# Eight zero fills that leave out one transfer engine in place of six, and four fills moved

## The chip, the cores and the metric

The kernel runs on one core of a Trainium2 chip. The metric is the device time of one launch in microseconds (us), here the median of several runs. The profiles show instructions of five engines (PE, here for matrix products, DVE, ACT, POOL and SP) and count transfers as a share of 16 transfer engines; in the kernel before these moved 248.19 MB, with 61.87 MB read from HBM and 185.60 MB written to it. All comparisons are between runs in the fast state, and the mean clock that the profiled runs were granted differs little (0.733 to 0.747 of full speed).

## The reference, cut to what matters

The program computes a decoder block with a modulated layer norm, attention over the last 4096 positions of a 65,536-long key and value cache, and a gated feed-forward part (FFN), and then all its gradients. The gradients of the two caches are nearly all zeros:

```python
k = jnp.repeat(k_cache[:, :, Sk - W:, :], rep, axis=1)   # W = 4096 of Sk = 65536
v = jnp.repeat(v_cache[:, :, Sk - W:, :], rep, axis=1)
# ... attention, FFN ...
_out, _vjp = jax.vjp(_f, A_x, A_k_cache, A_v_cache, A_wq, ...)
_grads = _vjp(grad_out)     # dK and dV have the caches' full size; rows before Sk - W are zero
```

So the kernel must write 2 x 4 x 61,440 x 128 zeros in bf16. That is 120 pieces of 1 MB (128 rows of 8 KB each), about half of all that it moves. Nothing waits for these zeros, so they can be written at any time.

## The kernel before

Python lists say how many zero fills are issued at which place. `NARROW` says which fills, by their index in the order of issue, are narrow.

```python
SKIP = 4
NARROW = (8, 20, 40, 65, 90, 104)
Z_Q = [0] * 7 + [3]                    # after the products of q, tile j
Z_N = spread(29, 128)                  # N stage, paced by PE and DVE
Z_B = spread(29, 43) + [1, 1, 1, 1, 0] # B stage, paced by PE
Z_FOLD = (3, 4)
Z_FFN = [(1, 1, 1, 1)] * 6 + [(1, 2, 1, 1)]   # seven FFN blocks, four places each
Z_END = (3, 1, 1, 1, 1)                # gradient stage at the end; what is left comes last
...
def zero(n, after=None):
    for _ in range(n):
        ...
        region, narrow_ = zleft.pop(0)
        if narrow_:
            nc.gpsimd.inc_swdge_sem([], [], mode="reset_dge_cursor")
            ...
            first = nc.gpsimd.dma_start(      # NS = SKIP + 1 = 5 rows: ten packets of 256 bytes
                out=rest[0:NS, ...], in_=zeros[0:NS, 0:64]...)
            ins = nc.gpsimd.dma_start(        # 120 rows = 60 x 2: 120 packets of 8 KB
                out=region[8:P, :]..., in_=zeros[0:60, :]...)
        else:
            ins = nc.gpsimd.dma_start(out=region.bitcast(FP32), in_=zeros[:, :])  # 128 rows
```

A wide fill is 128 packets of 8 KB, a narrow one 120. The packet records name no engine, but a fill's packets are followed by 4-byte ones. In before the narrow fill 104 ends with fifteen of these, at 462.72 to 464.37 us. The wide fill after it ends with sixteen: one at 466.01 us, the other fifteen at 467.06 to 468.71 us. So I read it that a wide fill gives each of the 16 transfer engines 8 packets, and a narrow one gives 15 of them 8 packets and one none. The 8 rows that each narrow fill leaves out are written early by one transfer (`zero_rest`; 128 packets of 2,880 bytes at 62.7 to 64.4 us in before), but for a few columns of them, which the leading writes and one small transfer take.

Block q of the FFN, with the places of its fills z[0] to z[3]:

```python
for j in range(KD):
    ...                                   # DVE and ACT products
    if j == 3: store_ug(q, 0, 4); zero(z[0])
    if j == 5: store_ug(q, 4, 2)
store_ug(q, 6, 2); zero(z[1])
...front, gates of block q + 1...
wd_ttr(q + 1, 0); load_ug(q + 2, 0, 4)
wd_outer(q + 1, 0); zero(z[2])            # wd_outer ends with the store of dW_down
...
wd_outer(q + 1, 1); load_ug(q + 2, 6, 2); zero(z[3])
load_wd(q + 2, 0); load_wd(q + 2, 1)
```

## Time and profile before

| | before |
|---|---|
| median time | 611.87 us (611.64 to 614.99; the three runs known before the prediction, 612.51 with three later ones) |
| moved | 248.19 MB, mean 406 GB/s |
| busy share PE, DVE, ACT, POOL | 64%, 53%, 46%, 29% |
| next-to-last transfer engine done | 605.00 us |
| last transfer engine done | 608.45 us |

The last two rows are read from the packet records of the trace: the 4-byte packets that end the fills and stores were sorted by time. After the one that ends at 605.00 us, all that is left are eleven 8 KB packets one behind the other, every 0.30 us, and two more of 4 bytes, the last of which ends at 608.45 us. The page's list of queues shows who uses the transfer engines (queue, kind: packets, MB, share of the 16 engines' span), and its next line what HBM saw:

```profile
q0 software_dynamic: 37696, 210.78, 89.5%
q1 hardware_dynamic: 11632, 36.71, 17.4%
q8 instruction: 35, 0.57, 0.4%
...
HBM read 61.87 MB, written 185.60 MB: 405 GB/s over the span
```

The reader is to see q8: 0.57 MB of instructions, counted against the same 16 engines as the data. This looks like nothing as a share of 16 engines (0.4%). As a share of one engine, which moves 248.19 / 16 = 15.5 MB in all, it is 3.7%.

### The profile page before, as it was taken

The page shows a single profiled execution, that of the slowest core. Times are in us where ns is not written, and L with a number is a line of the kernel's source. Part 1 is how long each engine was busy: PE and PEld are TensorE (multiplying, and loading weights), DVE is VectorE, ACT ScalarE, POOL GpSimd, SP SyncE. Part 2 cuts the span into 40 slices and gives each one's busy share as a digit, 9 for nine tenths or more (in the row PEclk, how much of TensorE's full clock was granted, in tenths as well). Part 3 has the DMA queues.
Part 4 walks back from the last instruction along what each step waited for, and adds up shares of the span by engine and source line. Part 5 has one row for each costly group of instructions (what it writes and reads, how often), then busy time and mean ns, then how long its engine had stood idle before and what let it go on. Part 6 is the DMA issues. An engine that isn't in the chain of part 4 may idle for free.

```text
span 611.6 us, 10920 instructions
## 1 busy us (share of the span) xinstructions
PE 390.4 (64%) x4516; PEld 267.5 (44%) x4516; DVE 325.4 (53%) x616; ACT 282.5 (46%) x426; POOL 176.3 (29%) x279
## 2 busy tenths in 40 slices
PE   3997789999999989899542444534333666944200
PEld 3995434334345546448432433423332355834200
DVE  2654589999401020160564695666747378785600
ACT  3489515557301024127281965837548525943100
POOL 0002121221222211213432456454443333222320
PEclk9999799999999989988655555555555576555555
DMA  8999999999999999999999999999999999999995
GB/s 351 420 419 359 400 424 412 412 416 418 422 423 424 427 427 421 415 416 397 395 418 412 393 398 414 408 409 412 409 414 351 424 416 414 424 425 426 425 424 221
DMA packets 49426, 248.19 MB, mean 406 GB/s; under 512 B 5517, under 2 KB 5517, under 8 KB 28944
## 3 DMA queue, kind: packets, MB, share of 16 engines
q0 software_dynamic: 37696, 210.78, 89.5%
q1 hardware_dynamic: 11632, 36.71, 17.4%
q8 instruction: 35, 0.57, 0.4%
q14 instruction: 15, 0.12, 0.1%
q10 hardware_dynamic: 48, 0.01, 0.0%
HBM read 61.87 MB, written 185.60 MB: 405 GB/s over the span
## 4 chain that ended last, share of the span: by engine, by line
PE 37%; DMA 30%; DVE 14%; ACT 8%; issue 6%; POOL 1%; ACTq 0%; POOLq 0%; DVEq 0%; SPq 0%
DMA out_dram<-arena 15%; PE b_ps L688 14%; DMA arena<-in_B_w_down_dram 9%; PE n_ps L636 6%; DVE arena L194 4%; DVE arena L207 4%; DMA out_dram<-zeros 4%; DVE junk L211 3%; ACT arena L242 2%; PE t_ps L598 2%; PE fold_ps L883 2%; ACT arena L838 2%; PE w_ps L395 2%; PE tp_wq L454 2%; PE tp_k L435 1%
## 5 line engine op out<-in xcount | busy, mean ns | idle before, releaser
L170 POOL DMA_DIRECT2D out_dram<-zeros x114 | 64.0, 563 | 206.7 <-PE q_ps L472 52.2
L688 PE MATMUL b_ps<-arena 128*128 128x512 bf16 x384 | 90.0, 390 | 0.0
L837 PE MATMUL tp_side<-ident_bf,arena 128*128 128x128 bf16 x416 | 50.2, 297 | 51.5 <-ACT arena L838 41.9
L838 ACT COPY arena<-tp_side 128x1024 bf16<-128x1024 bf16 x52 | 52.2, 1010 | 55.4 <-PE tp_side L837 55.2
L194 DVE TENSOR_TENSOR arena<-arena 128x2048 bf16<-128x2048 bf16 x64 | 76.6, 1223 | 2.3 <-PE n_ps L636 0.3
L211 DVE CUSTOM_DVE_ANT_0 arena<-arena,scr 128x1024 bf16<-128x1024 bf16 x56 | 65.2, 1223 | 9.4 <-ACT scr L970 9.4
L636 PE MATMUL n_ps<-arena 128*128 128x512 bf16 x256 | 65.8, 378 | 6.4 <-DVE arena L194 4.7
L837 PEld LDWEIGHTS <-arena 128*128 128x128 bf16 x416 | 41.0, 137 | 56.2 <-issue 56.1
L242 ACT ACTIVATE arena<-scr,h 128x1024 bf16<-128x1024 bf16 x56 | 61.0, 1145 | 0.0
L688 PEld LDWEIGHTS <-arena 128*128 128x128 bf16 x384 | 37.9, 101 | 46.8 <-issue 7.9
L211 DVE CUSTOM_DVE_ANT_0 junk<-arena,b1k 128x1024 bf16<-128x1024 bf16 x28 | 34.3, 1224 | 25.4 <-DMA arena<-in_B_w_down_dram 24.9
L874 POOL DMA_DIRECT2D out_dram<-arena x42 | 30.7, 732 | 50.4 <-ACT arena L242 43.3
L636 PEld LDWEIGHTS <-arena 128*128 128x128 bf16 x256 | 24.6, 97 | 41.7 <-issue 16.4
L1135 ACT ACTIVATE arena<-ps_kv 128x512 bf16<-128x512 f32 x48 | 26.2, 687 | 29.3 <-PE ps_kv L1131 28.8
L1131 PE MATMUL ps_kv<-junk,arena 8*128 8x128 bf16 x256 | 27.1, 303 | 14.4 <-DVE arena L207 13.3
L600 ACT CAST arena<-t_ps 128x512 bf16<-128x512 f32 x56 | 30.1, 589 | 12.1 <-PE t_ps L598 12.1
L950 PE MATMUL fg<-hh_bf,arena 128*128 128x1 bf16 x224 | 8.0, 166 | 39.3 <-DMA arena<-in_B_w_down_dram 37.5
L1131 PEld LDWEIGHTS <-arena 8*128 8x128 bf16 x256 | 25.2, 140 | 16.1 <-issue 16.1
L203 DVE CAST arena<-b_ps 128x512 bf16<-128x512 f32 x5 | 3.5, 692 | 47.0 <-PE b_ps L688 47.0
L456 ACT COPY arena<-tp_wq 128x1024 bf16<-128x1024 bf16 x23 | 21.8, 1032 | 8.3 <-PE tp_wq L454 8.3
L950 PEld LDWEIGHTS <-arena 128*128 128x128 bf16 x224 | 7.1, 105 | 42.2 <-DMA arena<-in_B_w_down_dram 40.1
L207 DVE TENSOR_SCALAR arena<-arena,cs_col 128x4096 bf16<-128x4096 bf16 (+1 forms) x16 | 16.1, 1024 | 11.2 <-DMA out_dram<-arena 10.9
(297 smaller groups left out, 649.0 us busy)
## 6 DMA issues: line engine op xcount, KB each, us to landing
out_dram<-zeros POOLq DMA_DIRECT2D x114, 1024.0 KB, 14.5
out_dram<-arena POOLq DMA_DIRECT2D x32, 1024.0 KB, 18.2
out_dram<-arena POOLq DMA_DIRECT2D x36, 512.0 KB, 8.9
arena<-in_A_wq_dram SPq DMA_DIRECT2D x8, 1024.0 KB, 19.9
arena<-in_B_w_down_dram SPq DMA_DIRECT2D x14, 512.0 KB, 10.6
out_dram<-arena POOLq DMA_DIRECT2D x28, 256.0 KB, 9.2
arena<-in_A_wo_dram SPq DMA_DIRECT2D x6, 1024.0 KB, 24.8
arena<-in_w_mod_dram POOLq DMA_DIRECT2D x6, 1024.0 KB, 14.3
```

The costliest lines, as they stand in the source:

```text
L170: ins = nc.gpsimd.dma_start(out=region.bitcast(FP32), in_=zeros[:, :])
L194: return nc.vector.tensor_tensor(out=out, in0=a, in1=b, op=op)
L207: return nc.vector.tensor_scalar(out=out, in0=a, scalar1=s1, scalar2=None, op0=op0)
L211: return nc.vector.tensor_tensor_reduce(out=out, in0=w, in1=b, scale=1.0, scalar=0.0, op0=ALU.mult, op1=ALU.add, accum_out=acc)
L242: return nc.scalar.activation(out=out, in_=b, func=ACT.Copy, scale=col)
L600: nc.scalar.copy(out=o, in_=ps)
L636: mm = nc.tensor.matmul(nbank[k][:, :], lhsT=k_nat[:, g, t_ * DH:(t_ + 1) * DH], rhs=vp[:, t_ % 2, 4 * k:4 * k + 4, :].rearrange("p h d -> ...
L688: mm = nc.tensor.matmul(bbank[p][k][:, :], lhsT=a4[:, p, h, :], rhs=wo_t[u][:, a, k * 512:(k + 1) * 512], start=(i == 0 and a == 0), stop= ...
L837: nc.tensor.transpose(tp[:, i * P:(i + 1) * P], blk[:, i * P:(i + 1) * P], ident_bf[:, :])
L838: nc.scalar.copy(out=blk, in_=tp[:, :])
L874: nc.gpsimd.dma_start(out=ug_part(view, q, j0, n), in_=ug_tile(q, k, j0, n))
L1131: nc.tensor.matmul(ps[:, t4 * DH:(t4 + 1) * DH], lhsT=rows[32 * g:32 * g + HG, t_ * P:(t_ + 1) * P], rhs=hd[32 * g:32 * g + HG, :], start= ...
```

## The change

The intent is to fill the stretches in which the transfer engines run dry, and to level the load of the one engine that has more to do than the others.

```diff
-NARROW = (8, 20, 40, 65, 90, 104)
+NARROW = (8, 20, 35, 50, 65, 80, 95, 108)
-Z_Q = [0] * 7 + [3]
+Z_Q = [0] * 6 + [1, 3]
-Z_FFN = [(1, 1, 1, 1)] * 6 + [(1, 2, 1, 1)]
-Z_END = (3, 1, 1, 1, 1)
+Z_FFN = [(1, 1, 1, 1)] * 5 + [(1, 1, 2, 2), (2, 2, 1, 1)]
+Z_END = (2, 1, 1, 0, 0)
```

One fill goes from the very end to the Q stage, and three go from the end stage to FFN blocks 5 and 6. No compute instruction changes.

## The prediction

> **What bounds the kernel now.** I read the page first: the busy shares, then the slices. No compute engine is above 64% busy, while the DMA row is at 9 in nearly every slice.
>
> ```profile
> PE 390.4 (64%) x4516; PEld 267.5 (44%) x4516; DVE 325.4 (53%) x616; ACT 282.5 (46%) x426; POOL 176.3 (29%) x279
> ...
> DMA  8999999999999999999999999999999999999995
> GB/s 351 420 419 359 400 424 412 412 416 418 422 423 424 427 427 421 415 416 397 395 418 412 393 398 414 408 409 412 409 414 351 424 416 414 424 425 426 425 424 221
> DMA packets 49426, 248.19 MB, mean 406 GB/s; under 512 B 5517, under 2 KB 5517, under 8 KB 28944
> ```
>
> The kernel moves 248.19 MB, and 120 MB of it are zero fills that can be put anywhere in time. Good slices reach 424 to 427 GB/s; at 425 all bytes would take 584 us, and the mean of 406 makes them 611. So the time is that of the transfers plus whatever the transfer engines stand idle. The GB/s row shows where: slice 3 (46 to 61 us, 359) and slice 30 (459 to 474 us, 351) are the two dips inside, and the last slice is the tail. I then read these places by stretches (columns: stretch, length, busy time of PE, weight load, DVE, ACT, POOL with counts, clock, DMA share, GB/s).
>
> ```profile
> 50.00:56.00 6.00, 4.84 (x97) 3.71 (x95) 1.37 (x4) 5.97 (x9) 2.00 (x4) 1.00 0.66 262
> 56.00:60.00 4.00, 2.82 (x38) 1.61 (x35) 3.40 (x7) 4.00 (x8) 1.74 (x3) 1.00 1.14 426
> 466.00:470.00 4.00, 1.01 (x8) 0.85 (x8) 4.00 (x7) 4.00 (x5) 1.51 (x3) 0.50 0.57 210
> 470.00:476.00 6.00, 2.02 (x16) 1.70 (x16) 1.04 (x7) 4.90 (x6) 4.42 (x7) 0.50 1.05 375
> 598.00:603.00 5.00, 0.00 (x0) 0.00 (x0) 0.00 (x0) 0.00 (x0) 0.00 (x0) 0.50 1.13 433
> 603.00:605.10 2.10, 0.00 (x0) 0.00 (x0) 0.00 (x0) 0.00 (x0) 0.00 (x0) 0.50 0.54 197
> 605.10:608.50 3.40, 0.00 (x0) 0.00 (x0) 0.00 (x0) 0.00 (x0) 0.00 (x0) 0.50 0.07 24
> ```
>
> The reader is to see two holes with full rate after them, and at the end 3.4 us at 24 GB/s in which no engine computes. 433 GB/s over 16 engines is 27 GB/s each, so 24 is one transfer engine working alone: 15 are done by about 605, one ends at 608.45. In the packet records an 8 KB packet recurs every 0.3035 us on an engine, so the late one has some eleven packets left when the next-to-last stops.
>
> Why one engine is late shows in the queue list of the tail (470 to 612 us):
>
> ```profile
> q8 instruction: 7, 0.11, 0.3%
> q14 instruction: 4, 0.03, 0.1%
> ```
>
> Seven packets of 16 KB. At 27 GB/s each is 0.607 us, together 4.25 us, about the lag of the late engine: after the hole at 468 us all 16 start level, and 3.45 us (against the next-to-last) build up in 140 us. Over the whole kernel q8 has 35 such packets (0.57 MB), 21.2 us of one engine. That they all lie on one engine is my inference from this fit. The narrow fills, which leave one engine out (120 rows instead of 128), pay it back: 8 packets each, 2.43 us, and 2.6 with what the other 15 take on. Six give 15.5 us of 21.2, eight 20.7.
>
> [...] The records have no engine number, so no view shows which one is left out. [...]
>
> **The change, part by part.** No compute instruction changes. The listing of POOL against before gives what moves.
>
> Q stage: Z_Q gains one fill after the j=6 products. These end at 50.07 us; from issue to first packet a fill took 1.2 us here (54.00 to 55.23), so it runs from 51.3, beside the last V loads, into the hole. The hole lacks (426-262) x 6 us = 0.98 MB; the fill brings 1.05 MB. It fits, and one fill less has to go at the end: 1.05 MB at 425 GB/s is 2.45 us, less the startup and the overlap with the V loads, say 2.2 us. The middle stages (56 to 280 us) are paced by PE and DVE with a fixed number of fills, so I take it that they are not moved.
>
> FFN: three more fills, and three fewer in the end stage before the last one. What POOL issues around the hole:
>
> ```profile
> 454.17 0.61 POOL L163 DMA_DIRECT2D out_dram<-zeros  x1
> 456.60 0.67 POOL L166 DMA_DIRECT2D out_dram<-zeros  x1 [1.81 <-DMA out_dram<-arena]
> 459.99 0.75 POOL L860 DMA_DIRECT2D out_dram<-arena  x1 [2.72 <-DVE arena L207]
> 460.73 0.58 POOL L170 DMA_DIRECT2D out_dram<-zeros  x1
> 468.49 1.51 POOL L874 DMA_DIRECT2D out_dram<-arena  x2 [7.18 <-ACT arena L242]
> ```
>
> Two fills before a 7.18 us wait for ACT's outer products; the queue runs dry at 468. After the change four fills stand there: 2 x 2.45 = 4.9 us of work against a hole of (420-210) x 4 + (420-375) x 6 = 1.1 MB, 2.6 us. The hole closes with 2.3 us of queue to spare. I count 2.1 us. The loads for block 6 have landed by 455.7, so nothing that compute waits for is held up. The third extra fill (block 6) only lies earlier.
>
> End stage: before issues 9 fills from Z_END on (7 and a rest of 2), after 5 (4 and 1). Stores must feed the engines with less padding. DVE ends at 579.8 and PE and ACT before 580, while the last transfer ends at 608.45; POOL's issues from 533 on mostly wait for landings, and a 1 MB store takes 18.2 us from issue to landing, seven transfers deep. Taking out two fills between 533 and 555 costs 5 us of that depth at most: it stays busy.
>
> Narrow fills: two more. If no engine ran dry from the B stage on, the late engine would gain 5.2 us and the tail would go: 3.4 us. But both narrow fills of the FFN only change places (90 and 104 become 95 and 108), the added ones lie earlier (four in N and B become six), and an engine that gets ahead loses that wherever the queue runs low, as in 270 to 340 us (single 2 us bins of 320 to 370 GB/s). Also the hole at 468, which closes, was what let the late engine catch up. I count 1.3 us of 3.4.
>
> Cost: the rows that narrow fills leave are written once by a spread transfer, 64 KB each, so 131 KB more: 0.3 us. [...]
>
> Sum: -2.2 -2.1 -1.3 +0.4 = -5.2 us, from 611.87 to 606.7.
>
> **The rivals.** First, the fill in the Q stage delays V loads and PE's instruction fetch (PE waits 0.9 us at 52.3), and the N stage, which is paced by compute, starts later: the 2.2 us are lost, 609. For it: the fetch at 50.8 took 1.07 us and shares an engine. Against: V is first read near 69 us. Second, lag takes the place of the hole: with no catching up at 468 the late engine carries its FFN lag into the end and the tail grows to some 5 us: 609 to 610. For it: q8 makes 10 fetches in the FFN (6.1 us) against two narrow fills (5.2). Third, the opposite: balance is complete and shorter landings also speed up the weight waits of the FFN (the chain has w_down loads at 9%): 602 to 604. Against: in the FFN the sixteen completions of a load lie within 1.5 us for several engines, not for one late one. Fourth, the end stage starves: up to +4 us, unlikely by the depth above.
>
> **Range and chances.** The terms give 603.5 if all succeed and 610.5 if two fail; the three runs of before spread by 3.4 us with one outlier. Over 2% faster needs 599.6, more than both holes and the tail together (2.3+2.6+3.4 = 8.3, to 603.6): 3%. Over 2% slower needs a new wait of 12 us in unchanged compute: 1%.
>
> **What would show it.** Right: 50 to 56 us above 380 GB/s, no dip below 400 near 466 to 470, and at the end less than 3 us with one engine alone. If both holes are closed but the one-engine tail is 4 us or more, the second rival holds. If the rate sags between 500 and 600 us, the fourth. If the holes close and the N stage begins later than 73.2 us, the first.

## More of the kernel before

A later section needs one more view of before, the stretch from 330 to 337 us (length, busy time of PE, weight load, DVE, ACT and POOL with counts, clock, share of the transfer engines, GB/s):

```profile
330.00:337.00 7.00, 2.50 (x32) 2.08 (x33) 4.44 (x12) 1.82 (x3) 3.35 (x5) 0.50 1.10 407
```

Here the transfers run at 407 GB/s, against 424 to 427 in the good slices.

## The result, and the profile after

The changed kernel took 607.33 us in the median (606.83 to 607.43, six runs), the kernel before 612.51 us (611.64 to 614.99, six runs). The ratio is 0.9911 (95% interval 0.9893 to 0.9929). Ratios are computed from the mean time of one kernel's fast runs over that of the other's of the same rounds, so they are not quite the ratio of the medians quoted. The interval says that it is a real gain of 0.7 to 1.1%.

The page of the changed kernel has these lines for what was shown of before:

```profile
GB/s 353 419 417 421 409 426 413 413 419 420 420 425 426 424 426 419 402 425 411 403 412 391 374 396 409 407 416 404 409 414 420 420 423 411 421 424 425 426 416 282
DMA packets 49522, 248.19 MB, mean 410 GB/s; under 512 B 5629, under 2 KB 5629, under 8 KB 29056
...
HBM read 61.87 MB, written 185.60 MB: 409 GB/s over the span
```

The two inner dips are gone (slice 3 has 421, slice 30 has 420), and a new one is at slice 22 (374). The bytes are the same to the last digit. The stretches of the changed kernel, with the columns as before:

```profile
50.00:56.00 6.00, 4.77 (x90) 3.21 (x88) 2.17 (x5) 5.97 (x9) 2.68 (x5) 1.00 1.21 419
330.00:337.00 7.00, 3.40 (x55) 2.88 (x53) 6.40 (x14) 2.02 (x2) 2.71 (x4) 0.50 0.78 294
466.00:470.00 4.00, 1.01 (x8) 0.85 (x8) 4.00 (x7) 4.00 (x5) 0.43 (x1) 0.50 1.09 418
470.00:476.00 6.00, 1.73 (x16) 1.56 (x16) 2.12 (x9) 5.24 (x6) 4.82 (x8) 0.50 1.12 419
600.00:602.00 2.00, 0.00 (x0) 0.00 (x0) 0.00 (x0) 0.00 (x0) 0.00 (x0) 0.50 0.45 164
602.00:604.00 2.00, 0.00 (x0) 0.00 (x0) 0.00 (x0) 0.00 (x0) 0.00 (x0) 0.50 0.03 8
```

The first, third and fourth lines show both holes closed. The second is the new dip: 294 GB/s where before had 407. The last two show the tail: after 602 us only 8 GB/s x 2 us = 16 KB are left, two packets, where before moved one engine's worth of data for 3.45 us.

What POOL issues around the former hole (start, length, line and what is moved; in brackets the idle time before and what ended it) shows how it was closed:

```profile
461.78 0.55 POOL L169 DMA_DIRECT2D out_dram<-zeros  x1
462.32 0.59 POOL L162 DMA_DIRECT2D out_dram<-zeros  x1
462.91 0.66 POOL L165 DMA_DIRECT2D out_dram<-zeros  x1
469.57 1.55 POOL L873 DMA_DIRECT2D out_dram<-arena  x2 [6.00 <-ACT arena L241]
```

POOL still waits 6 us for ACT's outer products, a little later than before (469.57 in place of 468.49). But it has put more into the queue ahead of that wait, so the transfer engines do not notice.

Where the time went can be summed up by the work the engines did not do. For each stretch I take its length less the bytes moved in it over 427 GB/s, the rate of the good slices (worked out from the packet records):

| stretch | lost before, us | lost after, us | gain |
|---|---|---|---|
| 50 to 60 us (Q stage) | 2.38 | 0.14 | 2.24 |
| 325 to 350 us (FFN block 1) | 1.76 | 3.32 | -1.56 |
| 460 to 480 us (FFN block 6) | 2.83 | 0.22 | 2.61 |
| 596 us to the last byte | 4.15 | 1.78 | 2.37 |
| all other stretches | | | 0.29 |
| last byte | 608.45 | 602.50 | 5.95 |

The profiled runs differ by 6 us, the medians by 5.2 us. Three of the stretches are those of the prediction; the fourth, a new dip, is not.

### The profile page after: what moved, and what is told of

It reads as the page before. It is cut to its first block, busy times and chain, and to the rows that moved or that the text cites.

```text
span 605.6 us, 10906 instructions
## 1 busy us (share of the span) xinstructions
PE 388.1 (64%) x4496; PEld 265.6 (44%) x4516; DVE 325.1 (54%) x616; ACT 282.4 (47%) x426; POOL 177.8 (29%) x281
## 3 DMA queue, kind: packets, MB, share of 16 engines
HBM read 61.87 MB, written 185.60 MB: 409 GB/s over the span
## 4 chain that ended last, share of the span: by engine, by line
PE 35%; DMA 29%; DVE 17%; ACT 8%; issue 7%; POOL 1%; ACTq 0%; POOLq 0%; another core or an unknown queue 0%; DVEq 0%; SPq 0%
DMA out_dram<-arena 15%; PE b_ps L687 14%; DMA arena<-in_B_w_down_dram 9%; PE n_ps L635 6%; DVE arena L206 4%; DVE arena L193 4%; DMA arena<-in_B_w_gate_dram 3%; DVE arena L210 3%; DVE junk L210 3%; ACT arena L241 2%; PE t_ps L597 2%; DMA arena<-in_B_w_up_dram 2%; PE tp_wq L453 2%; PE w_ps L394 2%; PE tp_k L434 1%
## 5 line engine op out<-in xcount | busy, mean ns | idle before, releaser
L169 POOL DMA_DIRECT2D out_dram<-zeros x112 | 61.6, 550 | 203.8 <-PE q_ps L471 50.4
L687 PE MATMUL b_ps<-arena 128*128 128x512 bf16 x372 | 88.2, 389 | 0.6
```

The source lines that it names most:

```text
L687: mm = nc.tensor.matmul(bbank[p][k][:, :], lhsT=a4[:, p, h, :], rhs=wo_t[u][:, a, k * 512:(k + 1) * 512], start=(i == 0 and a == 0), stop= ...
```

## The experiments

Twelve kernels ran, in three groups, each timed in five rounds against the kernel before on the same chip (its median was 612.94, 612.89 and 613.00 us). All outputs are right. Where a run is set against the changed kernel, the kernel before moves by 0.5 us between them (612.51 to 613.00), so no difference below that is read. "Alone" is the time between the end of the next-to-last transfer engine and that of the last, from the completion packets. The three GB/s columns are means over stretches.

| run | median, us | ratio to before (95%) | alone, us | 50 to 60 | 330 to 337 | 466 to 470 |
|---|---|---|---|---|---|---|
| before | 612.51 | 1 | 3.45 | 328 | 407 | 210 |
| after | 607.33 | 0.9911 (0.9893 to 0.9929) | 0.06 | 422 | 294 | 418 |
| n1_narrow_only | 610.55 | 0.9969 (0.9954 to 0.9983) | 1.54 | 383 | 403 | 182 |
| n2_fills_only | 606.76 | 0.9903 (0.9890 to 0.9915) | 0.44 | 421 | 284 | 424 |
| n3_q_fill_only | 611.83 | 0.9982 (0.9970 to 0.9994) | 3.65 | 422 | 332 | 251 |
| n4_ffn_fills_only | 608.35 | 0.9927 (0.9915 to 0.9938) | 0.67 | 362 | 364 | 427 |
| n5_narrow_80_to_74 | 607.15 | 0.9898 (0.9877 to 0.9920) | 0.15 | 419 | 298 | 420 |
| n6_without_108 | 609.29 | 0.9934 (0.9912 to 0.9955) | 3.01 | 422 | 284 | 424 |
| n7_other_engine | 615.54 | 1.0035 (1.0014 to 1.0057) | 5.49 | 418 | 248 | 417 |
| n8_extra_refills | 610.22 | 0.9948 (0.9924 to 0.9972) | 2.39 | 420 | 309 | 420 |
| n9_before_without_104 | 612.21 | 0.9988 (0.9973 to 1.0003) | 3.53 | 356 | 368 | 181 |
| n10_only_108 | 612.19 | 0.9985 (0.9971 to 0.9999) | 3.81 | 420 | 262 | 417 |
| n11_fill_in_block0 | 606.29 | 0.9887 (0.9870 to 0.9905) | 0.14 | 424 | 404 | 408 |
| n12_six_and_fill | 606.64 | 0.9897 (0.9880 to 0.9913) | 1.16 | 421 | 398 | 418 |

### The change taken apart

**Narrow fills alone** (everything else as before):

```diff
-NARROW = (8, 20, 40, 65, 90, 104)
+NARROW = (8, 20, 35, 50, 65, 80, 95, 108)
```

> The eight narrow fills alone, fills where they were before (two stay in a row at 475 us, so the last narrow one is issued after the 468 us hole). Theory (separate terms): both holes stay open, the one-engine tail of 3.4 us shrinks to under 1.5 us (gain about 2.4 us), but a narrow fill among the four fold fills costs POOL one more landing and opens a loss of about 1.5 us near 330 us; sum: 0.5 to 1.5 us faster than before. Rival (balance is what the change is about): 4 us faster or more, as much as the whole change less the Q hole.

It is 0.31% faster, 1.9 us, a little more than the 0.5 to 1.5 us expected. The hole at 468 us stays (182 GB/s) and the time alone falls from 3.45 to 1.54 us, nearly as expected (under 1.5). The expected dip near 330 us did not come (403 GB/s): that part of the theory fails here, and with it the loss that it was to bring.

**Moved fills alone**, with the six old indices:

```diff
-NARROW = (8, 20, 35, 50, 65, 80, 95, 108)     # of the changed kernel
+NARROW = (8, 20, 40, 65, 90, 104)
```

> The shifted fills alone, six narrow ones at their old indices. Theory: both holes closed (2.2 + 2.6 us), nothing lost near 330 us because no narrow fill is among the fold fills, tail of one engine stays at 2 to 4 us: 4 to 5 us faster than before. Second rival of the prediction (lag takes the hole's place): tail grows to 5 us or more and the gain is 2 to 3 us.

This is the surprise. It gains 0.97%, all that the whole change gains. The time alone is 0.44 us, not 2 to 4: with both holes closed, six narrow fills level the end as well as eight. The expected absence of the dip near 330 us is wrong too (284 GB/s), so that dip does not come from where the narrow fills are.

**The Q fill alone:**

```diff
-Z_Q = [0] * 7 + [3]
+Z_Q = [0] * 6 + [1, 3]
```

> Only the one fill moved into the Q stage. Theory: 2.2 us faster than before (50 to 60 us at over 410 GB/s in place of 326). Rival (V loads or instruction fetch delayed, N stage later): 0 to 1 us.

It gains 0.18%, 1.1 us, between the two theories. The hole closes (422 GB/s), so the fill does what it should. Two things make it worth less than 2.2 us. The hole was deeper in the profile of before than in other runs with the same code there: 328 GB/s, but 383, 362 and 356 in the three runs without the Q fill. And a part is given back at 330 to 337 us, where the rate is 332.

**The FFN and end fills alone:**

```diff
-Z_FFN = [(1, 1, 1, 1)] * 6 + [(1, 2, 1, 1)]
-Z_END = (3, 1, 1, 1, 1)
+Z_FFN = [(1, 1, 1, 1)] * 5 + [(1, 1, 2, 2), (2, 2, 1, 1)]
+Z_END = (2, 1, 1, 0, 0)
```

> Only the FFN and end fills moved. Theory: the hole at 466 to 472 us closes, 2 to 2.6 us faster than before. Rival (the tail of one engine grows because nothing lets it catch up): 0 to 1 us faster, tail over 4.5 us.

It gains 0.73%, 4.5 us, twice what was expected. The hole gives the 2.6 us, and besides the time alone falls from 3.45 to 0.67 us although the narrow fills are the old six. The rival, a longer tail, is refuted with the opposite sign. The two fill runs add up: 1.1 + 4.5 is near the 6 us of both together.

### Which engine, and what loads it

**Another engine left out** (the leading write of a narrow fill has 3 rows in place of 5):

```diff
-SKIP = 4
+SKIP = 2
```

> The changed kernel with the narrow fills leaving out another engine (the leading write has 3 rows in place of 5[...]). Theory: [...] one engine ends alone by 4 us or more (8 x 2.6 us of relief missing, less what holes and the queue depth forgive), the kernel slower than the changed one by 4 us or more and slower than the kernel before. Rival (which engine is left out does not matter): same as the changed kernel.

The kernel is 8.2 us slower than the changed one and slower than before. Its tail, in the columns of the stretches:

```profile
604.00:606.00 2.00, 0.00 (x0) 0.00 (x0) 0.00 (x0) 0.00 (x0) 0.00 (x0) 0.50 0.14 49
606.00:608.00 2.00, 0.00 (x0) 0.00 (x0) 0.00 (x0) 0.00 (x0) 0.00 (x0) 0.50 0.06 27
608.00:610.00 2.00, 0.00 (x0) 0.00 (x0) 0.00 (x0) 0.00 (x0) 0.00 (x0) 0.50 0.07 27
610.00:612.00 2.00, 0.00 (x0) 0.00 (x0) 0.00 (x0) 0.00 (x0) 0.00 (x0) 0.50 0.02 8
```

The two middle lines hold exactly one engine's rate, 27 GB/s. So it matters how many rows the leading write has: with 5 one engine is alone for 0.06 us, with 3 for 5.49 us. With 5, then, the narrow fills spare the engine that has more to do. That they spare another one with 3 is my reading of the times; the packet records name no engine.

**Five more instruction refills** at the end of the changed kernel:

```diff
     zero(len(zleft))
+    pad_ps = new_acc("pad_ps")
+    for _ in range(640):
+        nc.tensor.matmul(pad_ps[:, 0:1], lhsT=ident_bf[:, :], rhs=ident_bf[:, 0:1], start=True, stop=True)
```

> The changed kernel with 640 products of 128x1 nobody reads at the very end of PE's program: 1280 instructions more, five more 16 KB refills (40 in place of 35), while PE is otherwise idle after 576 us. Theory: all refills lie on one engine, 5 x 0.607 = 3.0 us more for it; it ends alone, the kernel 1.5 to 3 us slower than the changed one. Rival (refills spread over the engines or are hidden): within 0.4 us.

The time rises by 2.9 us (607.33 to 610.22), against 5 x 0.607 = 3.0 us worked out. The list of queues and the new tail:

```profile
q8 instruction: 40, 0.66, 0.4%
```

```profile
602.00:604.00 2.00, 0.33 (x13) 0.32 (x13) 0.00 (x0) 0.00 (x0) 0.00 (x0) 0.50 0.12 43
604.00:606.00 2.00, 1.86 (x70) 1.78 (x67) 0.00 (x0) 0.00 (x0) 0.00 (x0) 0.50 0.07 20
```

Forty packets in place of 35 for 1,280 more instructions of PE, and one engine alone for 2.39 us. If the refills were spread over the engines, five would have cost 3.0 / 16 = 0.2 us. So these refills lie on one engine, and it is the late one. The extra products could be a rival cause by their own time, because PE ends with them:

```profile
603.67 2.19 PE L1285 MATMUL pad_ps<-ident_bf 128*128 128x1 bf16 x77 [4.02 <-issue]
```

They end at 605.86 us, 0.37 us after the last byte of data (605.49), so at most 0.4 us of the loss can be theirs. No transfer of data waits for them, and the last byte of data itself came 2.99 us later than in the changed kernel (602.50).

### When a narrow fill counts

**The last narrow fill of the changed kernel made wide:**

```diff
-NARROW = (8, 20, 35, 50, 65, 80, 95, 108)
+NARROW = (8, 20, 35, 50, 65, 80, 95)
```

> The changed kernel with seven narrow fills, the last one (108) made wide. Theory: one transfer engine has 2.4 us more after 465 us; it ends alone, 1.5 to 2.5 us after the others, and the kernel is 1.5 to 2.2 us slower than the changed one. Rival (the level end has another cause, as the filled hole): within 0.5 us of the changed kernel.

It is 2.0 us slower than the changed kernel (609.29 against 607.33), as the theory says, and one engine is alone for 3.01 us, somewhat longer than the 1.5 to 2.5 us expected.

**The last narrow fill of the kernel before made wide:**

```diff
-NARROW = (8, 20, 40, 65, 90, 104)
+NARROW = (8, 20, 40, 65, 90)
```

> The kernel before with its last narrow fill (104, issued at 456 us, landed before the hole at 468 us) made wide. Theory: at the hole all sixteen engines wait for new work, so what the narrow fill saved its engine is thrown away; the time is within 0.7 us of before and the one-engine tail the same 3 to 4 us. Rival (the credit is kept, as it is with the hole closed, where leaving out 108 cost 2.1 us): 1.5 to 2.5 us slower than before.

The same edit on the other kernel costs nothing: 0.9988, an interval that holds 1, and 3.53 us alone against 3.45. Fill 104 was issued at 456 us and landed (464.37 us) just before the queue ran dry at 468. The engine that it spared 2.4 us of work (8 x 0.3035) ended the next fill at 466.01 us, the others at 467.06 to 468.71, and there was no other work for it to take up. When all sixteen then wait for POOL, whose next issue comes at 468.49 us, they start level again, and the seven refills after 470 us (4.25 us by the prediction's estimate) build up the whole lag anew, 3.45 us. The packet records show it: the last data before the hole land at 468.76 us, and all sixteen engines end the first transfer after it between 471.36 and 471.58 us. The run with the FFN and end fills alone is the counterpart: the same six indices, 104 issued at 455.4 us, but no hole after it, and 0.67 us alone. So in the kernel before, this narrow fill was wasted by the hole, and closing the hole put it to work.

**Only the last narrow fill kept:**

```diff
-NARROW = (8, 20, 35, 50, 65, 80, 95, 108)
+NARROW = (108,)
```

> The changed kernel with one narrow fill alone, the last (108). Theory: the early ones only keep the late engine from lagging through the N, B and FFN stages; without seven of them its lag (10 refills from 56 to 282 us, 6 us, and 6 more in the FFN) delays the FFN's load and store landings, and is partly wiped where the queue runs dry: 3 to 9 us slower than the changed kernel. Rival (only what comes after the last dry spell counts): within 1 us of the changed kernel.

It takes 612.19 us, 4.9 us more than the changed kernel, within the theory's range. The early ones are needed too. By sums like those of the table above, 2.7 us of the loss lie after 596 us, where one engine is alone for 3.81 us, and 1.3 us at 325 to 350 us, where the rate at the dip falls to 262 GB/s. That a late engine delays landings there, which the FFN waits for, would explain the second part; it is not shown.

Side by side, the runs suggest what sets the tail: the number of narrow fills issued after the last stretch in which the queue ran dry. With the hole at 468 us open and none after it, one engine is alone for 3.45, 3.65 and 3.53 us (before, n3, n9); with one after it, for 1.54 (n1). With that hole closed the dip at 330 to 337 us is the last such stretch: two narrow fills after it leave 0.06, 0.44 and 0.67 us (after, n2, n4), one leaves 3.01 and 3.81 (n6, n10), and n7, in which by the reading above none spares the late engine, leaves 5.49. This would be why six narrow fills did as well as eight: both lists have two after the dip (90 and 104, or 95 and 108). It is a reading of finished runs, not a forecast that one of them tested.

### The new dip

**The sixth narrow fill moved six places earlier:**

```diff
-NARROW = (8, 20, 35, 50, 65, 80, 95, 108)
+NARROW = (8, 20, 35, 50, 65, 74, 95, 108)
```

> The changed kernel with its sixth narrow fill six fills earlier, out of the stretch (295 to 305 us) where POOL waits for a landing before each issue. Theory: the small leading write of a narrow fill takes an issue slot of its own, 2.4 us there; without it the w_down store of block 0 is issued near 304 to 305 us in place of 307.5 and the hole of 1.5 us at 331 to 336 us closes: 1 to 1.6 us faster than the changed kernel (ratio to before about 0.988 to 0.989). Rival (the hole comes from the fill order or the load, not from the narrow fill): same time as the changed kernel, hole still there.

My theory falls. The w_down store of block 0 was indeed issued earlier (306.01 us in place of 307.50), and the dip stays all the same (298 GB/s). The time is that of the changed kernel.

**One more fill ahead of the dip:**

```diff
-Z_FFN = [(1, 1, 1, 1)] * 5 + [(1, 1, 2, 2), (2, 2, 1, 1)]
+Z_FFN = [(1, 2, 1, 1)] + [(1, 1, 1, 1)] * 4 + [(1, 1, 2, 2), (2, 2, 1, 1)]
```

> The changed kernel with one more fill after block 0's stores (two in place of one), one less at the very end. Theory: the new dip at 331 to 336 us (0.78 MB missing) is a dry queue that one fill can close: 330 to 337 us goes from 294 to over 380 GB/s and the kernel is 1 to 1.8 us faster than the changed one (605.5 to 606.3). Rival (the fill in front holds up the w_down load or the loads behind it in POOL's order): no gain, or slower.

The dip closes:

```profile
330.00:337.00 7.00, 2.83 (x48) 2.30 (x48) 5.08 (x9) 1.46 (x2) 2.70 (x4) 0.50 1.12 404
```

The median is 606.29 us (605.93 to 606.43), 1.0 us below that of the changed kernel, the least that was expected, and every run is below every run of that kernel, though their ratios to before (0.9887 and 0.9911) have intervals that overlap. The dip is therefore a queue that runs dry, as the other two were. During it POOL stands for 9 us at one store (324.4 to 333.4 us in the changed kernel) that waits for DVE, which waits 10.90 us for the load of w_down (to 329.84 us). Why the queue runs dry here more in the eight runs with the Q fill and without the added fill (248 to 332 GB/s) than in the four without the Q fill (364 to 407) is not settled.

**The same with six narrow fills:**

```diff
-NARROW = (8, 20, 35, 50, 65, 80, 95, 108)
+NARROW = (8, 20, 40, 65, 90, 105)              # with the Z_FFN of the run before
```

> The same with six narrow fills (the old indices, the last one put to 105 so that it stays at the start of its place in block 5). Theory: the count of narrow fills above six is worth nothing once the holes are closed: within 0.6 us of the run before it, 1 to 1.8 us faster than the changed kernel. Rival (eight are needed when no hole lets the late engine catch up): 1.5 us or more slower than the run before it, with one engine ending alone.

Its median is 606.64 us, 0.35 us above the run before it, with 1.16 us alone. The theory holds within its 0.6 us; against the changed kernel the gain is 0.7 us in the medians, less than the 1 to 1.8 expected. A small use of the seventh and eighth narrow fill is not excluded.

## Why the prediction was right

The time was 607.33 us against 606.7 predicted, and the gain of 5.2 us is the predicted one. That the sum came out so well is luck: its errors cancelled. By its own steps:

- **"So the time is that of the transfers plus whatever the transfer engines stand idle."** Right. The bytes are unchanged, and the gain in the last byte is the sum of the idle stretches that went.
- **Q stage, 2.2 us.** The mechanism is right: the hole closes in every run with the fill. The size is off: alone it is worth 1.1 us. The term was sized from the one profile of before, whose hole was deeper than in three other runs, and a part came back as the new dip.
- **FFN, 2.1 us.** The hole was worth 2.6 us by the records. The step stopped there; it did not see that the closed hole also levels the end. Alone, these fills gave 4.5 us.
- **Narrow fills, 1.3 us: the step that failed.** It said that the hole at 468 us "was what let the late engine catch up", and gave the tail to the two added narrow fills. The runs show the reverse. The tail was 3.45 us with the hole and six narrow fills, 3.53 with the hole and five, and 0.67 without the hole and with six. The hole threw away the credit of fill 104. On top of the moved fills the new list of eight is worth nothing that could be measured (0.9903 without it, 0.9911 with it). Alone, with the hole open, it is worth 1.9 us; its last narrow fill is then issued at 474.7 us, after the hole.
- **Cost, 0.4 us.** The 0.3 us are not there. The rows that narrow fills leave out were counted twice: HBM was written 185.60 MB in both kernels. The other 0.1 us, for the leading writes, was an estimate of mine and is too small for any run here to show.
- **"That they all lie on one engine is my inference from this fit."** Borne out by two runs: five more refills cost 2.9 us, about what one engine needs for them (3.0), and a leading write of 3 rows in place of 5 cost 8.2 us.
- **Two figures.** The 35 packets fit PE's refills: the page counts 4,516 products and as many weight loads, 9,032 or 258 to a packet, and in n8 1,280 more instructions came with five more packets, 256 to each. The fills are 125.8 MB, not 120: 120 pieces of 1,048,576 bytes.
- **The rivals.** The first did not hold in its cause: the Q fill closed its hole and the loss came 280 us later. The sign set for it did appear, an N stage that begins after 73.2 us (74.11 in place of 73.09), but it does not mark the Q fill: N begins at 73.97 us in n1 without that fill and at 72.50 us in n2 with it. What differs is the product before N (`ok`), with 5.16 us at a mean granted clock of 0.69 after the change and 3.64 us at 1.00 before (clock of the stretch 69 to 74.1 us). The second is refuted by the fills alone. The third, complete balance, held for the tail but not for the FFN; the 1.5 us set against it are low, as the sixteen completions of a w_down load spread over 1.05 to 2.85 us in before (14 loads, six of them within 1.5 us). The fourth did not occur: from 500 to 550 us both kernels moved 420 GB/s.
- **Not foreseen:** the dip in FFN block 1, -1.56 us in the profile.

## What to carry to other kernels

Where transfers bound a kernel, look for the stretches in which their queue runs dry, and put work that nothing waits for ahead of the wait that causes them (one fill took the dip at 330 to 337 us from 294 to 404 GB/s); after each such move look for the next dry stretch. In these runs balance between the transfer engines was worth something only where no dry stretch followed: the last narrow fill was worth 2.0 us without a hole after it (n6), and nothing that could be measured with one (n9, 0.9988). So close the holes first and place the balancing transfers after the last one. Take a hole's worth from several runs rather than from one profile, and check that a small queue of another kind (here instructions, 0.4% of 16 engines) does not sit on one engine.
